# A pre-LN hedgehog attention and GeGLU block: statistics of one tile, transposes and applies moved between engines

## The chip, the cores and the metric

The kernel runs on one core of a Trainium2 chip. A core has TensorE (PE, matrix products and transposes), VectorE (DVE), ScalarE (ACT), GpSimd (POOL) and SyncE (SP, which here issues all the DMAs of the kernel's own code). Each engine works through its own list of instructions in order; engines wait for each other on semaphores. The metric is the device time of one execution in microseconds (us), as the median of several runs, lower is better.

## What is computed

The reference, cut to what matters. S = 2048 tokens, D = 640, H = 32 heads of Dh = 20, F = 1536, all bf16:

```python
x = A_x
h  = x + A_ref(layernorm(x), wqkv, w_phi, wo)
h2 = h + B_ref(layernorm(h), w_gate, w_up, w_down)
# A_ref
q, k, v = split(x @ wqkv)                         # H heads of 20
pq, pk = q @ w_phi[h], k @ w_phi[h]
phi_q = concat(softmax(pq), softmax(-pq))         # 40 features a head
phi_k = concat(softmax(pk), softmax(-pk))
kv, z = sum_s phi_k^T v, sum_s phi_k
o = (phi_q kv) / (phi_q z + 1e-6)
return o @ wo
# B_ref
return (gelu(x @ w_gate) * (x @ w_up)) @ w_down
```

There is no mask and no softmax over the sequence: the attention is linear, so kv and z are summed over all the tokens before the first query can be finished.

## The kernel before

The tokens are 16 tiles of 128, in four blocks of four (`x_sb[b]`). x is loaded, normalised (LN1) and transposed to `LN1T[b]`, which holds the features on the partitions; from it V, the K features and the Q features are made on TensorE. w_phi is folded into the K and Q weights on the chip: `BD` is w_phi set out as block diagonals, `fold` multiplies it with the transposed weights (`WkT`, `WqT`, transposed by DMA) and casts the product `wa` to `Wk2` or `Wq2`. All the code issues in program order, each engine keeping the order in which its instructions stand in the source; nothing is reordered. So a line moved in the source is moved in the list of each engine on which it issues something.

The opening (L249 to L440) brings the first tiles to the point where the loop can start. A layer norm has a statistics step, `ln_stats`: on DVE two `bn_stats` (L109) and a `bn_aggr` (L113) for each tile, then the reciprocal root of the variance, either on ScalarE as Ln and Exp (L118, L119, `log=True`) or on POOL as an addition and a power (L121, L122), and on POOL, where the apply is to be on ScalarE, the product mean times -rstd, `mr` (L127). Then there is an apply, on ScalarE (`ln_act`, L133) or on DVE (`ln_dve`, L138). The transposes are five on TensorE into a PSUM tile `tp` (L146), which ScalarE or DVE copies to LN1T (L147), or one DMA (L149). Tiles 0 and 1 (`CT`) are special: only their mean is subtracted (`xc`, L249) before the transposes, so that these need not wait for rstd, which comes in later as the scale of V's copy (`v_ev`, L292) and of K's exponentials (`k_tile`, L305; `nrstd` is -rstd). For the queries their part of LN1T is written again, normalised in full; this is the late apply in the loop's step 10. Tile 3's statistics come from ScalarE: `st3_act` makes the mean with an accumulating Identity and the sum of squares with an accumulating Square, and POOL makes the rstd (L377, L378); `ln_3` applies them on DVE. `warm` issues matmuls of ones. `v_part(t, c, ...)` multiplies feature blocks c of tile t with Wv.

The loop (L441 to L487) has one step for each tile t. Its order in a step:

- `k_tile(t)`: the K product `pk` on TensorE (L272), and on ScalarE the two exponentials `E` (L305, plus and minus).
- In steps 10 to 14 one `fold` of the query weights, whose cast to Wq2 is on ScalarE (L236).
- In steps 5, 9, 13 and 15 the sums kv of earlier tiles (`kv_tile`, `kvp`, L338).
- `v_mm(t + 4)`, the V product, then the apply of tile t + 6 on ScalarE with its DMA transpose, then the copy of V on ScalarE.
- In even steps the statistics of tiles t + 8 and t + 9, on DVE and POOL.
- `k_norm(t)`: on DVE the sums `sk` of the exponentials (L312) and their reciprocals `rs` (L316); then `vt` = V times rs for each of the two signs (L320), one on POOL and the other either on POOL at once (tiles in `VP` = 0, 2, 4, 6, 9, 11) or on DVE, one step later between that step's sk and rs (`todo`).
- In step 9 POOL sets up the masks (`KV`, `kmask`, L474 to L482). In step 10 the late apply of tiles 0 and 1, both on DVE, and their DMA transposes.
- In step 15 the query products of the first four groups, and their exponentials `Eq` (L363, L368). `QG` lists the groups: the number 5b + c stands for feature block c of token block b.

The last four tiles' `kv_tile` and the mask of kv end the loop. Then come the rest of the queries, attention (`attn_a` to `attn_e`: the products `ab` with KV, their copies `AB`, the division, Wo, the residual, LN2) and the FFN (`gate_up`, `down`), laid into each other by `weave`, which runs an attention step after a given number of FFN pieces.

PSUM tiles of the loop are taken from a pool `psG` of three buffers of two banks each: `pk`, `wa`, `pv` and `pq` in turn. So a product can begin when the one three before it has been read: for instance the wa of step 14 takes the buffer of step 13's pk, and the pk of step 15 that of step 13's wa.

Of the kernel before, what the change touches and what calls it, by code (L numbers as in the profile page):

```python
# [8 lines left out]
BF16 = mybir.dt.bfloat16  # L9
F32 = mybir.dt.float32  # L10
ALU = mybir.AluOpType
ACTF = mybir.ActivationFunctionType
# [5 lines left out]
def kernel(  # L18
# [12 lines left out]
    nc = tc.nc  # L31
    P = 128
    S = 2048
    D = 640
# [3 lines left out]
    NT = S // P  # L38
    NB = NT // 4
    NC = D // P  # L40
    NF = FF // P
    EPS = 1e-5
# [6 lines left out]
    LQ = (7, 8, 9, 9, 10)  # L49
    FQ = (10, 11, 12, 13, 14)  # L50

    QG = ((0, 1), (2, 3), (4, 5), (6,), (7, 8), (9, 10), (11, 12), (13, 14), (15,), (16,), (17,), (18,), (19,))
    QT = (15, 15, 15, 15)
    T3 = 3

# [11 lines left out]
    phi_v = A_w_phi.rearrange("h d f -> (h d) f")  # L67
# [8 lines left out]
    x_sb = [const.tile([P, 4, D], BF16, name=f"x_sb{b}") for b in range(NB)]  # L76
    wphi = const.tile([P, NC, Dh], BF16, name="wphi")
# [10 lines left out]
    nhalf = const.tile([P, 2], F32, name="nhalf")  # L88
# [52 lines left out]
    def transpose_to(dst, src, on_pe, on_dve=False):  # L141

        if on_pe:
            tp = psG.tile([P, 16, P], BF16, name="tp", tag="G")
            for c in range(NC):
                nc.tensor.transpose(tp[:, c, :], src[:, c * P:(c + 1) * P], ident)  # L146
            (nc.vector.tensor_copy if on_dve else nc.scalar.copy)(dst, tp[:, 0:NC, :])  # L147
        else:
            nc.sync.dma_start_transpose(dst, src)  # L149
# [7 lines left out]
    p1 = p1_cm.__enter__()  # L157
# [6 lines left out]
    fp = fp_cm.__enter__()  # L164
# [10 lines left out]
    nc.sync.dma_start(Wv[:, 0:2, :], w_v[:, 0:2, 2 * D:3 * D])  # L175
    nc.sync.dma_start(x_sb[0][:, 2:3, :], x_v[:, 2:3, :])
    nc.sync.dma_start(Wv[:, 2:4, :], w_v[:, 2:4, 2 * D:3 * D])
    nc.sync.dma_start(x_sb[0][:, 3:4, :], x_v[:, 3:4, :])
    nc.sync.dma_start(wphi, phi_v.rearrange("(c p) f -> p c f", p=P))
    nc.sync.dma_start(Wv[:, 4:5, :], w_v[:, 4:5, 2 * D:3 * D])  # L180
    nc.sync.dma_start(x_sb[1][:, 0:2, :], x_v[:, 4:6, :])

# [24 lines left out]
    def warm(*cols):  # L207
        for n in cols:
            nc.tensor.matmul(wu[:, 0, 0:n], lhsT=ones[:, 0:P], rhs=ones[:, 0:n], start=True, stop=True)
# [30 lines left out]
    lnp, Ek, Vt = {}, {}, {}  # L240
# [4 lines left out]
    def ln_0(t):  # L245
        xt, mean, rstd, _ = lnp[t] = ln_stats(p1, [x_sb[0][:, t, :]], f"c{t}", False, None, True)[0]
        nc.gpsimd.tensor_scalar(nrstd[t], rstd, -1.0, None, op0=ALU.mult)
        xc = fp.tile([P, D], BF16, name="xc", bufs=2)
        nc.vector.tensor_scalar(xc, xt, mean, None, op0=ALU.subtract)  # L249
        return xc  # L250

    def ln_st(*tiles, act=True, between=None, log=False):
        for t, v in zip(tiles, ln_stats(p1, [x_sb[t // 4][:, t % 4, :] for t in tiles], "1", act, between, log)):
            lnp[t] = v

    def ln_ap(t, on_act=False, on_pe=False):
        ln = (ln_act if on_act else ln_dve)(p1, "1", *lnp[t])
        if on_pe:
            lnp[t] = ln
        else:  # L260
            transpose_to(LN1T[t // 4][:, :, t % 4 * P:(t % 4 + 1) * P], ln, False)
# [20 lines left out]
    def v_part(t, *cs):  # L282

        if 0 in cs:
            pv[t] = gtile("pv")
        for c in cs:
            for u in range(2):
                nc.tensor.matmul(pv[t][:, u, 0:HD], lhsT=lnT(t, c), rhs=Wv[:, c, u * HD:(u + 1) * HD],
                                 start=(c == 0), stop=(c == NC - 1))
# [10 lines left out]
    def k_tile(t):  # L300
        pk = gtile("pk")
        proj(pk, t, Wk2, rows=t == 0)
        Ek[t] = ev.tile([P, 2, D], BF16, name="E", bufs=8)
        for s in range(2):
            nc.scalar.activation(Ek[t][:, s, :].rearrange("p (u f) -> p u f", u=2), pk[:, :, 0:HD],  # L305
                                 ACTF.Exp, scale=((lnp[t][2], nrstd[t]) if t in CT else (1.0, -1.0))[s])
# [60 lines left out]
        for s in signs:  # L367
            nc.scalar.activation(Eq[j][:, :, s, :], pqs[j][:, 0:len(QG[j])], ACTF.Exp, scale=(1.0, -1.0)[s])  # L368

    def st3_act(i):  # L370

        xt = x_sb[0][:, 3, :]
        if i == 0:
            nc.scalar.activation(sq3, xt, ACTF.Identity, scale=-1.0 / D, accum_out=v3[:, 0:1])
        else:
            nc.scalar.activation(sq3, xt, ACTF.Square, bias=v3[:, 0:1], accum_out=v3[:, 1:2])
            nc.gpsimd.tensor_scalar(v3[:, 2:3], v3[:, 1:2], 1.0 / D, EPS, op0=ALU.mult, op1=ALU.add)  # L377
            nc.gpsimd.tensor_tensor(v3[:, 3:4], v3[:, 2:3], nhalf[:, 0:1], op=ALU.pow)  # L378

    def ln_3():  # L380

        ln = lnp[3] = p1.tile([P, D], BF16, name="ln1", bufs=3)
        nc.vector.tensor_scalar(ln, x_sb[0][:, 3, :], v3[:, 0:1], v3[:, 3:4], op0=ALU.add, op1=ALU.mult)

    sq3 = fp.tile([P, D], BF16, name="sq3")
    v3 = fp.tile([P, 4], F32, name="v3")

    def bd(c0, c1):

        n = c1 - c0  # L390
        nc.vector.tensor_tensor(BD[:, c0:c1], wphi[:, c0:c1, None, :].to_broadcast([P, n, 8, Dh]),
                                hmask[:, c0:c1, :, None].to_broadcast([P, n, 8, Dh]), ALU.mult)

    def tr_c(t):
        transpose_to(LN1T[0][:, :, t * P:(t + 1) * P], xc[t], True, t == 1)

    xc = [ln_0(t) for t in CT[:1]]
    tr_c(0)
    xc.append(ln_0(1))
    warm(*[P] * 7)  # L400
    ln_st(2, act=False, log=True)
    v_part(0, 0, 1)
    tr_c(1)
    st3_act(0)
    v_part(0, 2, 3)
    ln_ap(2, on_pe=True)
    bd(0, NC)
    st3_act(1)
    v_part(1, 0, 1)
    ln_tp(2, True)  # L410
    v_part(1, 2, 3)
    v_part(0, 4)
    v_ev(0)
    v_part(1, 4)
    v_ev(1)
    ln_st(4, act=False)
    ln_3()
    v_part(2, *range(NC))
    v_ev(2)
    nc.sync.dma_start(x_sb[1][:, 2:4, :], x_v[:, 6:8, :])  # L420
# [21 lines left out]
    for t in range(NT):  # L442
        if t == T3:
            ps_cm.close()
            psG = ps_cm.enter_context(tc.tile_pool(name="psG", bufs=3, space=PSUM, reuse_waits="tile"))
            psK = ps_cm.enter_context(tc.tile_pool(name="psK", bufs=1, space=PSUM, reuse_waits="tile"))
            kvp = psK.tile([P, 2, 512], F32, name="kvp")
        k_tile(t)
        if t == 0:
            ln_ap(6)  # L450
        if t in FQ:
            fold(WqT, Wq2, True, [i for i, f in enumerate(FQ) if f == t])
        for j in range(len(QT)):
            if t == QT[j]:
                q_mm(j)
                q_exp(j)
        for i in KVG.get(t, ()):
            kv_tile(i)
        if 0 < t < NT - 4:
            v_mm(t + 4)  # L460
        if t > 0 and t + 6 < NT:
            ln_ap(t + 6, on_act=True)
        if 0 < t < NT - 4:
            v_ev(t + 4)
        if t % 2 == 0 and t + 8 < NT:
            ln_st(t + 8, t + 9)
        k_norm(t)
        load_T(WqT, 0, *[i for i, f in enumerate(LQ) if f == t])
        if t == 10:

            for i in CT:
                ln_ap(i)
        if t == 9:
            nc.gpsimd.memset(KV, 0.0)  # L474
            nc.gpsimd.memset(kmask, 1.0)
            for r in HALF:
                nc.gpsimd.affine_select(out=kmask[r], in_=kmask[r], pattern=[[4, NC], [-Dh, 4]],
                                        compare_op=ALU.is_ge, fill=0.0, base=0, channel_multiplier=1)
                nc.gpsimd.affine_select(out=kmask[r], in_=kmask[r], pattern=[[-4, NC], [Dh, 4]],
                                        compare_op=ALU.is_ge, fill=0.0, base=Dh - 1, channel_multiplier=-1)  # L480
            nc.gpsimd.tensor_copy(KV[:, :, 0, :, KC - 1], kmask)
            nc.gpsimd.tensor_copy(KV[:, :, 1, :, 0], kmask)  # L482
        if t == 13:
            nc.sync.dma_start(Wg, wg_v)
            nc.sync.dma_start(Wo, wo_v)
            nc.sync.dma_start(Wu, wu_v)
# [60 lines left out]
    def attn_a(t, dve=0):  # L547
        attn_a_mm(t)
        AB, ab = ABs[t % 2], st[t, "ab"]
        for u in ((1, 0) if t in (5,) else (0, 1)):  # L550
            (nc.vector.tensor_copy if u >= 2 - dve else nc.scalar.copy)(
                AB[:, :, u * UH:(u + 1) * UH].rearrange("p s h f -> p s (h f)"), ab[u][:, :, 0:UH * KC])
        st[t] = AB
# [215 lines left out]
    def attn_at(t, i, offs):  # L769

        fns = (attn_a, attn_b, attn_b2, attn_b3, attn_c, attn_d, attn_d2, attn_e)
        return [(i + o, fn, t) for fn, o in zip(fns, offs) if o >= 0]
# [5 lines left out]
    def attn_rest(t, i):  # L778
# [2 lines left out]


    weave(gus(0, 0, 256) + downs(0, (0, 1)),
          attn_at(2, 0, (-1, 0, 1, 2, 7, 7, 8, 10)) + attn_at(3, 1, (1, 2, 3, 4, 9, 9, 10, 12)) + attn_at(4, 6, SHORT2) + attn_at(5, 9, SHORT2) +
          attn_at(6, 13, SHORT2))
    weave(gus(0, 256, 512) + downs(0, (2, 3)),
          attn_at(7, 0, SHORT) + [(12, split), (14, attn_pair, 8), (16, attn_pair, 10)] + attn_rest(8, 15) +
# [37 lines left out]
```

## Time and profile before

| what | us |
|---|---|
| median of 3 runs | 277.09 (276.90 to 277.39) |
| the profiled execution | 277.39 |
| its span in the trace | 275.5 |
| opening, to the first pk | 0 to 16.56 |
| loop and end of kv | 16.56 to 70.3 |
| attention of all tiles and FFN | 70.3 to 275.5 |

The span is what the trace shows from the first to the last instruction; the 1.9 us between it and the execution's time lie around it. Times in the profile count from the span's start. The granted TensorE clock is 1.00 in the whole span by the records. Busy times of the engines by stretch, in us:

| stretch | TensorE | DVE | ScalarE | POOL |
|---|---|---|---|---|
| 0 to 6.2 | 5.34 | 3.64 | 2.52 | 2.78 |
| 6.2 to 16.55 | 10.30 | 8.66 | 7.50 | 2.65 |
| 16.55 to 70.3 | 53.24 | 51.35 | 45.69 | 40.63 |
| 70.3 to 272.7 | 201.66 | 112.85 | 83.65 | 51.13 |

A line such as `26.95 0.23 POOL L121 TENSOR_SCALAR ve<-mv ... x1` reads: start, duration, engine, line of the kernel, operation, what it writes and reads; in brackets what the engine waited for just before and how long. A duration includes time in which the instruction has been issued but cannot go on, so the same operation may be recorded with two durations. DVE's instructions overlap a little: sk to rs is 1.47 from start to start, rs to the next 0.47, a vt 0.765.

### The profile page before, as it was taken

The page shows a single profiled execution, that of the slowest core. Times are in us where ns is not written, and L with a number is a line of the kernel's source. Part 1 is how long each engine was busy: PE and PEld are TensorE (multiplying, and loading weights), DVE is VectorE, ACT ScalarE, POOL GpSimd, SP SyncE. Part 2 cuts the span into 40 slices and gives each one's busy share as a digit, 9 for nine tenths or more (in the row PEclk, how much of TensorE's full clock was granted, in tenths as well). Part 3 has the DMA queues.
Part 4 walks back from the last instruction along what each step waited for, and adds up shares of the span by engine and source line. Part 5 has one row for each costly group of instructions (what it writes and reads, how often), then busy time and mean ns, then how long its engine had stood idle before and what let it go on. Part 6 is the DMA issues. An engine that isn't in the chain of part 4 may idle for free.

```text
span 275.5 us, 5930 instructions
## 1 busy us (share of the span) xinstructions
PE 270.5 (98%) x2335; PEld 174.2 (63%) x2348; DVE 176.8 (64%) x335; ACT 139.4 (51%) x239; POOL 97.2 (35%) x218
## 2 busy tenths in 40 slices
PE   8999999999999999999999999999999999999995
PEld 5777767765455887788764555675555576444574
DVE  6889999999495776675478773356866333333322
ACT  4879898869489755374552345223245510223100
POOL 4248897765202317365312553101165300000000
PEclk9999999999999999999999999999999999999999
DMA  7973526589820021316111142110123111000011
GB/s 207 194 236 61 73 53 104 80 261 393 273 87 0 4 50 35 85 49 70 32 48 48 26 69 51 38 61 2 48 47 71 26 48 50 25 0 0 0 50 48
DMA packets 42235, 21.37 MB, mean 78 GB/s; under 512 B 35040, under 2 KB 40416, under 8 KB 42208
## 3 DMA queue, kind: packets, MB, share of 16 engines
q1 hardware_dynamic: 42208, 21.01, 31.1%
q8 instruction: 18, 0.29, 0.5%
q14 instruction: 9, 0.07, 0.1%
HBM read 10.18 MB, written 2.62 MB: 46 GB/s over the span
## 4 chain that ended last, share of the span: by engine, by line
PE 72%; DVE 13%; issue 7%; SPq 4%; DMA 2%; ACT 1%; POOL 1%; DVEq 0%; ACTq 0%; POOLq 0%
PE gu L663 37%; PE pd L682 19%; PE po L603 8%; DVE sk L312 6%; PE pq L363 5%; DVE rs L316 3%; DVE stats L109 3%; PE ab L531 2%; SPq L186 2%; DMA x_sb<-in_A_x_dram 2%; POOL vt L320 1%; DVE vt L320 1%; PE tp L146 0%; ACT L666 0%; DVE mv L113 0%
## 5 line engine op out<-in xcount | busy, mean ns | idle before, releaser
L666 ACT ACTIVATE g<-gu 128x512 bf16<-128x512 f32 (+1 forms) x60 | 30.7, 512 | 68.6 <-PE gu L663 68.4
L669 DVE TENSOR_TENSOR GT<-gu,g 128x512 bf16<-128x512 f32 (+1 forms) x60 | 34.5, 580 | 47.9 <-PE gu L663 39.3
L663 PE MATMUL gu<-LN2T,Wg 128*128 128x512 bf16 (+1 forms) x291 | 61.3, 335 | 0.5
L663 PE MATMUL gu<-LN2T,Wu 128*128 128x512 bf16 (+1 forms) x300 | 61.7, 336 | 0.0
L682 PE MATMUL pd<-Wd,GT 128*128 128x320 bf16 (+2 forms) x396 | 53.5, 295 | 0.0
L682 PEld LDWEIGHTS <-GT 128*128 128x128 bf16 x396 | 37.9, 98 | 14.7 <-DVE GT L669 0.2
L663 PEld LDWEIGHTS <-Wu 128*128 128x128 bf16 x300 | 29.4, 98 | 22.6
L663 PEld LDWEIGHTS <-Wg 128*128 128x128 bf16 x300 | 28.8, 98 | 21.4
L272 PEld LDWEIGHTS <-LN1T 128*128 128x128 bf16 x290 | 27.7, 98 | 10.8 <-DMA LN1T<-ln 0.3
L685 DVE TENSOR_TENSOR y<-pd,x_sb 128x320 bf16<-128x320 f32 (+2 forms) x29 | 13.9, 480 | 29.0 <-PE pd L682 29.0
L320 POOL TENSOR_TENSOR vt<-vS,rs 128x672 bf16<-128x672 bf16 x22 | 29.1, 1344 | 9.1 <-DVE rs L316 8.8
L603 PE MATMUL po<-Wo,oT 128*128 128x320 bf16 x160 | 24.3, 299 | 0.0
L272 PE MATMUL pk<-Wk,LN1T 128*128 128x320 bf16 x160 | 24.2, 299 | 0.0
L363 PE MATMUL pq<-LN1T,Wq 128*128 128x512 bf16 x96 | 22.9, 379 | 0.2
L312 DVE TENSOR_REDUCE sk<-E 128x64 f32<-128x1280 bf16 x16 | 22.9, 1431 | 0.0
L368 ACT ACTIVATE Eq<-pq 128x1024 bf16<-128x1024 f32 (+1 forms) x26 | 20.0, 830 | 1.7 <-PE pq L363 1.7
L603 PEld LDWEIGHTS <-oT 128*128 128x128 bf16 x160 | 15.6, 98 | 7.4 <-ACT oT L147 0.5
L305 ACT ACTIVATE E<-pk 128x640 bf16<-128x640 f32 x28 | 18.2, 707 | 3.9 <-PE pk L272 3.8
L272 PE MATMUL pv<-Wv,LN1T 128*128 128x320 bf16 x130 | 19.8, 299 | 0.0
L580 DVE TENSOR_TENSOR tt<-AB,w 128x1280 bf16<-128x1280 f32 x12 | 17.9, 1488 | 1.1 <-POOL w L573 0.9
L133 ACT ACTIVATE ln<-x_sb,v,rstd 128x640 bf16<-128x640 bf16 x14 | 12.9, 920 | 10.7 <-POOL v L642 10.3
L363 PEld LDWEIGHTS <-Wq 128*128 128x128 bf16 x100 | 9.4, 98 | 10.0
(110 smaller groups left out, 294.3 us busy)
## 6 DMA issues: line engine op xcount, KB each, us to landing
out_dram<-y SPq DMA_DIRECT2D x15, 160.0 KB, 1.8
Wg<-in_B_w_gate_dram SPq DMA_DIRECT2D x1, 1920.0 KB, 7.8
Wu<-in_B_w_up_dram SPq DMA_DIRECT2D x1, 1920.0 KB, 12.5
Wd<-in_B_w_down_dram SPq DMA_DIRECT2D x1, 1920.0 KB, 8.2
x_sb<-in_A_x_dram SPq DMA_DIRECT2D x2, 640.0 KB, 6.1
Wo<-in_A_wo_dram SPq DMA_DIRECT2D x1, 800.0 KB, 9.4
x_sb<-in_A_x_dram SPq DMA_DIRECT2D x4, 160.0 KB, 2.9
Wv<-in_A_wqkv_dram SPq DMA_DIRECT2D x2, 320.0 KB, 3.9
```

Of the source, the lines that this page charges most:

```text
L272: nc.tensor.matmul(ps[:, u, 0:HD], lhsT=lnT(t, c), rhs=W[:, c, u * HD:(u + 1) * HD], start=(c == 0), stop=(c == NC - 1))
L305: nc.scalar.activation(Ek[t][:, s, :].rearrange("p (u f) -> p u f", u=2), pk[:, :, 0:HD], ACTF.Exp, scale=((lnp[t][2], nrstd[t]) if t in C ...
L312: nc.vector.reduce_sum(sk, Ek[t].rearrange("p s (h f) -> p (s h) f", f=Dh), axis=AX.X)
L320: eng.tensor_tensor(vt[:, s], vS[t % 8], rs[:, s * H:(s + 1) * H, None].to_broadcast([P, H, VC]), ALU.mult)
L363: nc.tensor.matmul(pqs[j][:, i, :], lhsT=Wq2[:, kc, c * P:(c + 1) * P], rhs=LN1T[b][:, kc, :], start=(kc == 0), stop=(kc == NC - 1))
L368: nc.scalar.activation(Eq[j][:, :, s, :], pqs[j][:, 0:len(QG[j])], ACTF.Exp, scale=(1.0, -1.0)[s])
L580: nc.vector.tensor_tensor(tt.rearrange("p s (h f) -> p s h f", f=Dh), num, w[:, :, :, None].to_broadcast([P, 2, H, Dh]), ALU.mult)
L603: nc.tensor.matmul(pos[u], lhsT=st[t][:, c, :], rhs=Wo[:, c, u * HD:(u + 1) * HD], start=(c == 0), stop=(c == NC - 1))
L663: nc.tensor.matmul(gu[i][:, 0:n], lhsT=W[:, c, f * P:(f + 1) * P], rhs=LN2T[b][:, c, a0:a1], start=(c == 0), stop=(c == NC - 1))
L666: nc.scalar.activation(g[:, 0:n], gu[0][:, 0:n], ACTF.Gelu_apprx_tanh)
L669: nc.vector.tensor_tensor(st[b, "g", f][:, a0:a1], gu[1][:, 0:n], g[:, 0:n], ALU.mult)
L682: nc.tensor.matmul(ps, lhsT=st[b, "g", f][:, tl * P:(tl + 1) * P], rhs=Wd[:, f, f0:f1], start=(f == 0), stop=(f == NF - 1))
```

## The change

The statistics of tile 1 move from DVE to ScalarE and POOL (`st_act`, the former `st3_act` for any tile, with `xc_a` and `ln_a` for its subtraction and its apply on DVE). The transposes of tiles 0 and 1 follow one another, both copied to LN1T by DVE; three of seven warming matmuls go; the V parts stand in another order; BD is built in two pieces; w_phi is loaded ahead of x of tile 3. In the loop the apply of tile t + 6 stands ahead of k_tile(t) from t = 2 on, and so ahead of its exponentials on ScalarE; the statistics of a pair come one step earlier from the second pair on (in steps 1, 3 and 5 in place of 2, 4 and 6). In step 10 only tile 1 is applied again on DVE; tile 0 is applied on ScalarE in step 12, with a product mean times -rstd that POOL makes in step 10 after its vt. The query group with feature blocks 5 and 6 comes first. In the weave, the attention steps of tile 3 begin one FFN piece later, and the two copies of `ab` are swapped for tile 4 where they were for tile 5.

```diff
@@ -49,7 +49,7 @@
     LQ = (7, 8, 9, 9, 10)
     FQ = (10, 11, 12, 13, 14)
 
-    QG = ((0, 1), (2, 3), (4, 5), (6,), (7, 8), (9, 10), (11, 12), (13, 14), (15,), (16,), (17,), (18,), (19,))
+    QG = ((5, 6), (0, 1), (2, 3), (4,), (7, 8), (9, 10), (11, 12), (13, 14), (15,), (16,), (17,), (18,), (19,))
     QT = (15, 15, 15, 15)
     T3 = 3
 
@@ -175,8 +175,8 @@
     nc.sync.dma_start(Wv[:, 0:2, :], w_v[:, 0:2, 2 * D:3 * D])
     nc.sync.dma_start(x_sb[0][:, 2:3, :], x_v[:, 2:3, :])
     nc.sync.dma_start(Wv[:, 2:4, :], w_v[:, 2:4, 2 * D:3 * D])
+    nc.sync.dma_start(wphi, phi_v.rearrange("(c p) f -> p c f", p=P))
     nc.sync.dma_start(x_sb[0][:, 3:4, :], x_v[:, 3:4, :])
-    nc.sync.dma_start(wphi, phi_v.rearrange("(c p) f -> p c f", p=P))
     nc.sync.dma_start(Wv[:, 4:5, :], w_v[:, 4:5, 2 * D:3 * D])
     nc.sync.dma_start(x_sb[1][:, 0:2, :], x_v[:, 4:6, :])
 
@@ -367,23 +367,31 @@
         for s in signs:
             nc.scalar.activation(Eq[j][:, :, s, :], pqs[j][:, 0:len(QG[j])], ACTF.Exp, scale=(1.0, -1.0)[s])
 
-    def st3_act(i):
-
-        xt = x_sb[0][:, 3, :]
+    def st_act(t, i):
+
+        xt, v = x_sb[0][:, t, :], va[t]
         if i == 0:
-            nc.scalar.activation(sq3, xt, ACTF.Identity, scale=-1.0 / D, accum_out=v3[:, 0:1])
+            nc.scalar.activation(sqa, xt, ACTF.Identity, scale=-1.0 / D, accum_out=v[:, 0:1])
         else:
-            nc.scalar.activation(sq3, xt, ACTF.Square, bias=v3[:, 0:1], accum_out=v3[:, 1:2])
-            nc.gpsimd.tensor_scalar(v3[:, 2:3], v3[:, 1:2], 1.0 / D, EPS, op0=ALU.mult, op1=ALU.add)
-            nc.gpsimd.tensor_tensor(v3[:, 3:4], v3[:, 2:3], nhalf[:, 0:1], op=ALU.pow)
-
-    def ln_3():
-
-        ln = lnp[3] = p1.tile([P, D], BF16, name="ln1", bufs=3)
-        nc.vector.tensor_scalar(ln, x_sb[0][:, 3, :], v3[:, 0:1], v3[:, 3:4], op0=ALU.add, op1=ALU.mult)
-
-    sq3 = fp.tile([P, D], BF16, name="sq3")
-    v3 = fp.tile([P, 4], F32, name="v3")
+            nc.scalar.activation(sqa, xt, ACTF.Square, bias=v[:, 0:1], accum_out=v[:, 1:2])
+            nc.gpsimd.tensor_scalar(v[:, 2:3], v[:, 1:2], 1.0 / D, EPS, op0=ALU.mult, op1=ALU.add)
+            nc.gpsimd.tensor_tensor(v[:, 3:4], v[:, 2:3], nhalf[:, 0:1], op=ALU.pow)
+            lnp[t] = xt, None, v[:, 3:4], None
+
+    def ln_a(t):
+
+        ln = p1.tile([P, D], BF16, name="ln1", bufs=3)
+        nc.vector.tensor_scalar(ln, x_sb[0][:, t, :], va[t][:, 0:1], va[t][:, 3:4], op0=ALU.add, op1=ALU.mult)
+        return ln
+
+    def xc_a(t):
+
+        xc = fp.tile([P, D], BF16, name="xc", bufs=2)
+        nc.vector.tensor_scalar(xc, x_sb[0][:, t, :], va[t][:, 0:1], None, op0=ALU.add)
+        return xc
+
+    sqa = fp.tile([P, D], BF16, name="sqa")
+    va = {t: p1.tile([P, 4], F32, name=f"va{t}") for t in (1, 3)}
 
     def bd(c0, c1):
 
@@ -392,29 +400,33 @@
                                 hmask[:, c0:c1, :, None].to_broadcast([P, n, 8, Dh]), ALU.mult)
 
     def tr_c(t):
-        transpose_to(LN1T[0][:, :, t * P:(t + 1) * P], xc[t], True, t == 1)
-
-    xc = [ln_0(t) for t in CT[:1]]
+        transpose_to(LN1T[0][:, :, t * P:(t + 1) * P], xc[t], True, True)
+
+    st_act(1, 0)
+    xc = [ln_0(0)]
+    xc.append(xc_a(1))
     tr_c(0)
-    xc.append(ln_0(1))
-    warm(*[P] * 7)
+    tr_c(1)
+    st_act(1, 1)
+    nc.gpsimd.tensor_scalar(nrstd[1], lnp[1][2], -1.0, None, op0=ALU.mult)
+    warm(*[P] * 4)
     ln_st(2, act=False, log=True)
     v_part(0, 0, 1)
-    tr_c(1)
-    st3_act(0)
+    v_part(1, 0, 1)
+    bd(0, 2)
+    st_act(3, 0)
     v_part(0, 2, 3)
     ln_ap(2, on_pe=True)
-    bd(0, NC)
-    st3_act(1)
-    v_part(1, 0, 1)
+    bd(2, NC)
+    st_act(3, 1)
+    v_part(1, 2, 3)
     ln_tp(2, True)
-    v_part(1, 2, 3)
     v_part(0, 4)
     v_ev(0)
     v_part(1, 4)
     v_ev(1)
     ln_st(4, act=False)
-    ln_3()
+    lnp[3] = ln_a(3)
     v_part(2, *range(NC))
     v_ev(2)
     nc.sync.dma_start(x_sb[1][:, 2:4, :], x_v[:, 6:8, :])
@@ -445,6 +457,8 @@
             psG = ps_cm.enter_context(tc.tile_pool(name="psG", bufs=3, space=PSUM, reuse_waits="tile"))
             psK = ps_cm.enter_context(tc.tile_pool(name="psK", bufs=1, space=PSUM, reuse_waits="tile"))
             kvp = psK.tile([P, 2, 512], F32, name="kvp")
+        if t > 1 and t + 6 < NT:
+            ln_ap(t + 6, on_act=True)
         k_tile(t)
         if t == 0:
             ln_ap(6)
@@ -458,18 +472,19 @@
             kv_tile(i)
         if 0 < t < NT - 4:
             v_mm(t + 4)
-        if t > 0 and t + 6 < NT:
-            ln_ap(t + 6, on_act=True)
+        if t == 1:
+            ln_ap(7, on_act=True)
         if 0 < t < NT - 4:
             v_ev(t + 4)
-        if t % 2 == 0 and t + 8 < NT:
-            ln_st(t + 8, t + 9)
+        if t == 0 or t % 2 and t + 9 < NT:
+            ln_st(t + 9 - (t == 0), t + 10 - (t == 0))
         k_norm(t)
         load_T(WqT, 0, *[i for i, f in enumerate(LQ) if f == t])
         if t == 10:
-
-            for i in CT:
-                ln_ap(i)
+            nc.gpsimd.tensor_scalar(lnp[0][3], lnp[0][1], nrstd[0], None, op0=ALU.mult)
+            transpose_to(LN1T[0][:, :, P:2 * P], ln_a(1), False)
+        if t == 12:
+            ln_ap(0, on_act=True)
         if t == 9:
             nc.gpsimd.memset(KV, 0.0)
             nc.gpsimd.memset(kmask, 1.0)
@@ -547,7 +562,7 @@
     def attn_a(t, dve=0):
         attn_a_mm(t)
         AB, ab = ABs[t % 2], st[t, "ab"]
-        for u in ((1, 0) if t in (5,) else (0, 1)):
+        for u in ((1, 0) if t in (4,) else (0, 1)):
             (nc.vector.tensor_copy if u >= 2 - dve else nc.scalar.copy)(
                 AB[:, :, u * UH:(u + 1) * UH].rearrange("p s h f -> p s (h f)"), ab[u][:, :, 0:UH * KC])
         st[t] = AB
@@ -781,7 +796,7 @@
 
 
     weave(gus(0, 0, 256) + downs(0, (0, 1)),
-          attn_at(2, 0, (-1, 0, 1, 2, 7, 7, 8, 10)) + attn_at(3, 1, (1, 2, 3, 4, 9, 9, 10, 12)) + attn_at(4, 6, SHORT2) + attn_at(5, 9, SHORT2) +
+          attn_at(2, 0, (-1, 0, 1, 2, 7, 7, 8, 10)) + attn_at(3, 1, (2, 3, 4, 5, 9, 9, 10, 12)) + attn_at(4, 6, SHORT2) + attn_at(5, 9, SHORT2) +
           attn_at(6, 13, SHORT2))
     weave(gus(0, 256, 512) + downs(0, (2, 3)),
           attn_at(7, 0, SHORT) + [(12, split), (14, attn_pair, 8), (16, attn_pair, 10)] + attn_rest(8, 15) +
```

## The prediction

> **What bounds the kernel now.** I read the engine shares first, then the chain of waits, then the timeline around the few waits that the chain shows. The page and the waits view:
>
> ```profile
> span 275.5 us, 5930 instructions
> PE 270.5 (98%) x2335; PEld 174.2 (63%) x2348; DVE 176.8 (64%) x335; ACT 139.4 (51%) x239; POOL 97.2 (35%) x218
> PE 72%; DVE 13%; issue 7%; SPq 4%; DMA 2%; ACT 1%; POOL 1%; DVEq 0%; ACTq 0%; POOLq 0%
> ...
> PE kvp L338 <- POOL vt L320: 0.5, 1, 0.5
> ```
>
> TensorE is busy for 98% of the span, so a gain has to remove TensorE time or a TensorE wait, and there is little of either. Yet 13% of the chain is DVE: in the K/V loop the chain runs on another engine. The chain's pieces at the two ends of the loop, and the timeline there:
>
> ```profile
> 11.93 4.59 DMA x_sb<-in_A_x_dram
> ...
> 67.15 0.55 DVE rs L316
> ...
> 67.86 1.98 POOL vt L320
> ...
> 16.55 0.89 DVE L109 BATCH_NORM_STATS2 stats<-x_sb 128x6 f32<-128x320 bf16 x2 [0.60 <-DMA x_sb<-in_A_x_dram]
> ...
> 69.88 0.38 PE L338 MATMUL kvp<-vt,E 128*64 128x84 bf16 x10 [0.45 <-POOL vt L320]
> ```
>
> The chain enters DVE at 16.55, when tiles 6 and 7 land, stays there to 67.15, and hands over to POOL's last vt, for which TensorE waits 0.45. From there on it is TensorE. So through the loop DVE and TensorE are level within 0.45 us: work that delays TensorE by d costs d − 0.45, and work that delays DVE and POOL costs all of it.
>
> Two engines that get in each other's way decide the rest. The timeline at tiles 1 and at 9 to 14:
>
> ```profile
> 26.95 0.23 POOL L121 TENSOR_SCALAR ve<-mv 128x2 f32<-128x2 f32 x1
> 27.82 0.85 DVE L320 TENSOR_TENSOR vt<-vS,rs 128x672 bf16<-128x672 bf16 x1
> ...
> 51.52 2.17 DVE L138 TENSOR_SCALAR ln<-x_sb,mvc,rstdc 128x640 bf16<-128x640 bf16 x2
> 52.27 0.83 POOL L474 MEMSET KV<- 128x880 bf16 x1
> ...
> 54.09 0.70 ACT L236 CAST Wq<-wa 128x640 bf16<-128x640 f32 x1
> 54.66 1.33 ACT L305 ACTIVATE E<-pk 128x640 bf16<-128x640 f32 x2
> 54.69 1.32 POOL L320 TENSOR_TENSOR vt<-vS,rs 128x672 bf16<-128x672 bf16 x1
> 55.00 1.72 DVE L320 TENSOR_TENSOR vt<-vS,rs 128x672 bf16<-128x672 bf16 x1
> 55.84 0.74 ACT L236 CAST Wq<-wa 128x640 bf16<-128x640 f32 x1
> 57.81 0.48 PE L227 MATMUL wa<-BD,WqT 128*128 128x140 bf16 x6
> ```
>
> A vt on DVE takes 0.85 alone (27.82) but 1.72 when POOL's vt is running (55.00): DVE stands until 0.13 before POOL's ends. The pair of L138 takes 2.17 against 0.43 each alone; it stood through a vt and a memset of POOL.
>
> **The change part by part.**
>
> *Opening* (tile 1's statistics on ScalarE, both transposes together, three warming matmuls fewer, another order of the V parts). Two bn_stats and one aggregate leave DVE (0.88 + 0.21); two accumulating ScalarE passes come (0.74 + 0.18 and 0.83 + 0.19, as tile 3's at 7.72 and 8.59), and POOL's scale and power (0.19 + 0.57). On TensorE the wait before tile 1's V parts (0.2 at 7.98) and three warms of 128 columns (0.107 each at the pace of that time) go, so tile 2's transposes come some 0.4 earlier. Then tile 3 is late. Its x is sent behind wphi (issue to issue 0.43 to 0.5: landing at about 8.2 for 7.70), its two ScalarE passes now stand behind tile 2's Ln and Exp and end at about 10.0, POOL's power at 10.9, DVE's L384 at 11.4, and its transposes start at 11.4 to 11.5 where they start at 11.26. That makes the first pk 0.1 to 0.25 late (16.56). DVE's chain starts with the landing at 16.52, whose issue at 11.93 stands on SP's queue behind the five transposes of WkT (5.20 to 11.89) as before, so it neither gains nor loses. TensorE's 0.1 to 0.25 goes into the wait found below. I count the opening as 0; without that cover it would cost up to 0.25, and its best end is −0.45, if TensorE gained 0.4 to the end of the opening and kept it.
>
> *Statistics of a pair one tile earlier* (10/11, 12/13, 14/15 before tiles 1, 3, 5). Nothing is added. But POOL's ve, rstd and two mr of the pair (26.95 to 29.03) now run ahead of its vt of tile 1 instead of during DVE's. Walk it from row starts: DVE's rs of tile 0 at 22.30; statistics to 24.5 (1.77, as at 24.70 to 26.47); sk and rs of tile 1 to 26.5; sk of tile 2 to 27.85. POOL: vt of tile 0 twice, 23.0 to 25.55; the four small ones 1.5, to 27.1; vt of tile 1 from 27.1 to 28.4. DVE's vt of tile 1, ready at 27.8, can start only at 28.25: 0.45 lost, where 27.82 shows none lost. The same walk gives 0.41 at tile 3 and 0.35 at tile 5. Sum 1.2; if each POOL piece is a little later, up to 0.65, 0.6, 0.5, which is 1.7; nothing is lost if DVE's instruction gets in first. DVE and POOL both reach tile 6 by s = 1.2 later. DVE has no idle time before there that could take it up.
>
> *ScalarE applies ahead of the exponentials.* Same instructions; the 0.92 of an apply (pitch 0.81) now stands before E, which waits for pk anyway. The next ln is one tile earlier, and the 0.74 that ScalarE stood at 41.52 for POOL's mr goes. ScalarE is 51% busy: I take 0 on the path.
>
> *Late apply.* Tile 1's stays on DVE (0.43, with its wait); tile 0's leaves DVE, 0.35 to 0.43 gained there, and comes on ScalarE at tile 12, between the Wq cast at 54.09 and the E pair of tile 13 at 54.66. It needs the new mean·(−rstd) of POOL, one small operation (0.24 to 0.26, as an mr), issued at tile 10 behind POOL's vt of that tile, which ran from 54.69 to 56.01. Even with the times of before: product done at 56.2, apply 56.25, E of tile 13 from 57.06 to 58.36 (it ended at 55.99), the Wq cast after it to 58.95 (56.58). TensorE's wa of tile 14 started at 57.81 into the buffer that this E frees: 0.55 late; pk of tile 15 at 58.12 into the buffer that the cast frees: 0.87 late. Against the 0.45 of TensorE's slack: +0.42, had POOL not been late. With s on POOL, 0.42 + 1.2 = +1.6. And there is a race: with s less the 0.35 to 0.43 saved, DVE's vt of tile 10 (55.00) asks at about 55.87, POOL's (54.69) at 55.90. If POOL wins, the sum stands at 1.6. If DVE wins, POOL waits 0.65 to 0.75 more, and all of that is in the product's time: 2.3. Of the two, 0.03 us apart, no row decides; I take the middle, 1.95.
>
> What is queued behind the waiting apply on ScalarE: both E of tile 13, the cast, then E of tiles 14 and 15. DVE's sk of tile 13 (59.10) waits for the first of these, and TensorE for all.
>
> [...] L138's first instruction, issued at 51.52 during POOL's vt, took 1.816: it stood not only through that vt, to 52.33, but through the memset that came after it, to 53.1. [...]
>
> *Order of the query groups, the weave of the first attention tiles.* The first q group now is one that does not read block 0, whose tile 0 is transposed about 3 us later than before (53.40 + 2.5); q starts after 60, so nothing waits. The KV readings of tile 3 move behind the third gate_up; TensorE lost 0.11 about 92.96, where the activation table's load and the first gelu hold it: −0.1, bounds −0.2 and +0.2.
>
> Sum: opening 0, statistics and late apply +1.95, weave −0.1: +1.85. The profiled execution took 277.39 with a span of 275.5 (1.9 around it); the median is 277.09, so the sum made against the span is put on the median: 277.09 + 1.85 = 278.94, say 279.0.
>
> **The rivals.**
> 1. *Faster, by the DVE work removed.* If the vts don't meet (DVE's gets in ahead of POOL's) and POOL's product is done by 54.8, DVE's chain loses 0.35 to 0.43, TensorE's wait of 0.45 shrinks with it, and opening and weave give 0.1 to 0.3: 277.09 − 0.45 − 0.2 = 276.4 to 276.6. For it: DVE has the longest unbroken stretch of the chain. Against it: POOL's vt of tile 10 ran to 56.01, 1.2 after ScalarE is free.
> 2. *No change.* The vts don't meet, but the product is late: +0.42 − 0.1, so 277.4.
> 3. *Slower, DVE the bound.* The apply is early enough after all, the vts meet: 1.2 − 0.4 = +0.8, so 277.9. It decides if the product is ready by 54.8 + s.
> 4. *Slower, the clock.* TensorE's pace goes from 107 to 56 ns per 128 columns between 6.45 and 6.68; with ten transposes in place of seven warms and five, the release could come later. V and pk up to 16.56 at half pace for another 1.3 or so, of which the wait above hides half: +0.7, so 279.7. [...]
>
> **How the numbers follow.** This kernel's runs differ by up to 0.2% (0.55 us), so "same" is 276.54 to 277.64. My forecast 0.58, rival 1 0.14, rival 2 0.12, rival 3 0.06, rival 4 0.10. Slower: 0.74; same 0.12; faster 0.14. The likeliest has 278.3 to 279.6 (1.6 and 2.3, 0.2 either way, and 0.3 for s up to 1.7). To leave out 2 in 10 at most, the range has to reach over rivals 2 to 4: 277.0 to 280.2.
>
> **What would show it.** In the timeline of after: ScalarE's L133 for tile 0 at about 57.5 to 58.3 with 2.5 us or more idle before it, released by POOL's L484; E of tile 13 ending at 59.6 to 60.4; TensorE's wa of tile 14 waiting two microseconds or more for ScalarE; kvp at the end of the loop no longer waiting for POOL. DVE's vt of tiles 1, 3, 5 recorded at 1.2 to 1.5 for 0.85. Tiles 6 and 7 still landing at 16.5; first pk at 16.65 to 16.8. It is wrong if the vts keep 0.85, if L484 runs before 55, or if ScalarE's apply starts with no wait.

## The result

The changed kernel takes 280.42 us (median of 4 runs, 280.30 to 281.36) against 277.00 for the kernel before beside it: a ratio of 1.0123, 95% interval 1.0108 to 1.0138. It is slower by 3.4 us, where the prediction said 1.9 and ended its range at 280.2. Two later comparisons of the same kernels gave 1.0129 (1.0097 to 1.0161) and 1.0139 (1.0119 to 1.0158); with more executions the kernel before had medians of 277.34 to 277.48, so 277.00 is at its low end. The profiled execution of the changed kernel took 281.36 with a span of 279.3, 3.8 more than the span before.

From the page of the changed kernel: the span, the busy times, and TensorE's granted clock in 40 slices of 7 us (tenths of full speed).

```profile
span 279.3 us, 5939 instructions
PE 272.8 (98%) x2345; PEld 174.4 (62%) x2345; DVE 176.3 (63%) x333; ACT 140.2 (50%) x241; POOL 96.7 (35%) x221
PEclk9999999988999999999999999999999999999999
```

TensorE's busy time rose by 2.3, though it has three matmuls less to do; and in the slices from 56 to 70 us the clock is down, where the page before has a 9 in every slice. The timeline of the changed kernel there, and below it the pk of the kernel before:

```profile
55.91 0.84 DVE L320 TENSOR_TENSOR vt<-vS,rs 128x672 bf16<-128x672 bf16 x1
55.94 1.98 POOL L320 TENSOR_TENSOR vt<-vS,rs 128x672 bf16<-128x672 bf16 x1
57.90 0.30 POOL L484 TENSOR_SCALAR mrc<-mvc,nrstd 128x1 f32<-128x1 f32 x1
58.24 0.92 ACT L133 ACTIVATE ln<-x_sb,mrc,rstdc 128x640 bf16<-128x640 bf16 x1 [3.38 <-POOL mrc L484]
59.07 1.27 ACT L305 ACTIVATE E<-pk 128x640 bf16<-128x640 f32 x2
60.39 0.47 PE L227 MATMUL wa<-BD,WqT 128*128 128x140 bf16 x6 [2.35 <-ACT E L305]
60.98 2.83 PE L272 MATMUL pk<-Wk,LN1T 128*128 128x320 bf16 x10
```

```profile
56.44 1.53 PE L272 MATMUL pk<-Wk,LN1T 128*128 128x320 bf16 x10
```

Read downward, the first block is the chain that the prediction described: DVE's vt of tile 10 came 0.03 us ahead of POOL's, POOL's took 1.98 instead of 1.31, the product (`mrc`) followed at 57.90, ScalarE had stood 3.38 for it, E of tile 13 came after the apply, and TensorE stood 2.35 for E. Its last line is the new thing: ten matmuls of pk took 2.83, where the same ten took 1.52 or 1.53 in the steps before it. The windows view of the changed kernel, with the stretch, its length, busy times and counts of TensorE, weight loads, DVE, ScalarE and POOL, then the granted clock:

```profile
57.00:64.60 7.60, 5.14 (x27) 2.79 (x26) 6.34 (x8) 5.22 (x9) 6.28 (x6) 0.78 0.49 128
61.00:64.40 3.40, 3.40 (x12) 1.70 (x12) 3.40 (x4) 2.27 (x4) 2.08 (x2) 0.51 0.83 221
```

For the 3.4 us after the wait TensorE had half its clock. From 60.98 to 63.60 ten matmuls of pk went at 267 ns from start to start (136 before), and the first pq until 64.4 at 376 to 427 ns (216): 1.6 us on top of the wait.

This is the profiled execution, and not every execution has it. Half the clock for 3.4 of 279 us by itself brings the mean granted clock of an execution to 0.994. Of the four executions measured here only the profiled one (281.36, span 279.3) has 0.994; the other three (280.30 to 280.48, spans 278.2 to 278.4) have 1.000. In the three measurements of the changed kernel together, 8 of 14 executions have 0.993 or 0.994, with a median of 281.5, and 6 have 1.000, with a median of 280.4. So the 280.42 is a time at full clock, and the clock is not what puts it above the forecast. Against 277.42, the median of 69 executions of the kernel before in the later measurements, the change costs 3.0 at full clock and 4.1 where the clock falls.

### The profile page after: what moved, and what is told of

Same layout as the page of the kernel before. It is cut to its first block, busy times and chain, and to the rows that moved or that the text cites. A ratio compares the mean times of both kernels' runs of the same rounds, so it can differ in the third digit from the quotient of the medians.

```text
span 279.3 us, 5939 instructions
## 1 busy us (share of the span) xinstructions
PE 272.8 (98%) x2345; PEld 174.4 (62%) x2345; DVE 176.3 (63%) x333; ACT 140.2 (50%) x241; POOL 96.7 (35%) x221
## 3 DMA queue, kind: packets, MB, share of 16 engines
HBM read 10.18 MB, written 2.62 MB: 46 GB/s over the span
## 4 chain that ended last, share of the span: by engine, by line
PE 77%; DVE 12%; issue 3%; POOL 3%; DMA 2%; ACT 2%; SPq 1%; DVEq 0%; POOLq 0%
PE gu L678 37%; PE pd L697 19%; PE pq L363 8%; PE po L618 8%; DVE sk L312 4%; DVE stats L109 3%; PE ab L546 3%; DVE rs L316 2%; DMA x_sb<-in_A_x_dram 2%; POOL vt L320 1%; PE pk L272 1%; PE kvp L338 1%; PE tp L146 1%; DVE vt L320 1%; DVE mv L113 1%
## 5 line engine op out<-in xcount | busy, mean ns | idle before, releaser
L272 PEld LDWEIGHTS <-LN1T 128*128 128x128 bf16 x290 | 28.3, 99 | 11.4 <-issue 0.2
L320 POOL TENSOR_TENSOR vt<-vS,rs 128x672 bf16<-128x672 bf16 x22 | 29.9, 1372 | 11.0 <-DVE rs L316 8.2
L272 PE MATMUL pk<-Wk,LN1T 128*128 128x320 bf16 x160 | 25.5, 310 | 0.1
```

Of the source, the lines that this page charges most:

```text
L272: nc.tensor.matmul(ps[:, u, 0:HD], lhsT=lnT(t, c), rhs=W[:, c, u * HD:(u + 1) * HD], start=(c == 0), stop=(c == NC - 1))
L320: eng.tensor_tensor(vt[:, s], vS[t % 8], rs[:, s * H:(s + 1) * H, None].to_broadcast([P, H, VC]), ALU.mult)
```

## The experiments

The loads of the opening landed at different times from run to run, so the loop began at different times with one and the same opening: BD's first piece, which needs w_phi, began at 7.20 without a wait in the run with both applies on DVE, at 7.93 after 0.28 of waiting for that load in the changed kernel and at 8.29 after 0.77 in the run with the early product. To compare loops, I read three starts in each trace: sk of tile 0 on DVE (where the loop's DVE chain begins), the end of E of tile 13, and the start of the last kvp matmul. The difference of the first and the last is the length of the loop, free of the opening.

| kernel | ratio to before, 95% interval | sk of tile 0 | E of 13 ends | last kvp | loop | E of 13 to last kvp |
|---|---|---|---|---|---|---|
| before | 1 | 20.83 | 55.99 | 70.06 | 49.23 | 14.07 |
| changed | 1.0123 (1.0108 to 1.0138) | 20.40 | 60.34 | 73.90 | 53.50 | 13.56 |
| changed, second time | 1.0129 (1.0097 to 1.0161) | 20.80 | 60.79 | 74.26 | 53.46 | 13.47 |
| changed, third time | 1.0139 (1.0119 to 1.0158) | 20.54 | 60.49 | 73.98 | 53.44 | 13.49 |
| product early | 1.0035 (1.0018 to 1.0052) | 20.91 | 57.18 | 71.10 | 50.18 | 13.92 |
| apply on DVE | 1.0052 (1.0029 to 1.0075) | 20.91 | 56.52 | 71.80 | 50.89 | 15.28 |
| statistics late | 1.0045 (1.0030 to 1.0061) | 20.21 | 58.47 | 70.39 | 50.18 | 11.92 |
| early product, late statistics | 1.0008 (0.9994 to 1.0021) | 21.71 | 58.27 | 70.89 | 49.19 | 12.62 |
| opening alone | 1.0013 (1.0001 to 1.0025) | 21.04 | 56.11 | 70.28 | 49.23 | 14.17 |
| old opening, rest repaired | 1.0006 (0.9993 to 1.0019) | 20.99 | 57.54 | 70.17 | 49.19 | 12.63 |
| filled wait | 1.0106 (1.0079 to 1.0132) | 21.47 | 61.41 | 73.33 | 51.86 | 11.92 |
| filled wait, second time | 1.0124 (1.0102 to 1.0145) | 20.53 | 60.51 | 72.42 | 51.89 | 11.91 |
| filled, no added tile | 1.0129 (1.0108 to 1.0149) | 21.86 | 61.79 | 73.71 | 51.86 | 11.92 |
| filled in part | 1.0104 (1.0084 to 1.0123) | 21.44 | 61.38 | 73.30 | 51.86 | 11.92 |

**The clock: matmuls of zeros in the wait.** Before the fold of step 14 in the changed kernel (`zeros` is a tile of its own, set to 0 by DVE in the opening):

```diff
+        if t == 14:
+            for i in range(14):
+                nc.tensor.matmul(kvp[:, 0, 0:420], lhsT=zeros[:, 0:P], rhs=ones[:, 0:420], start=False, stop=False,
+                                 skip_group_check=True)
```

> The changed kernel with 14 TensorE matmuls of zeros (420 columns, some 0.175 us each, 2.45 us in all, added to kvp as nothing) between the pk and the wa of step 14, where TensorE stood for 2.5 us. ScalarE's wait and the end of that wait stay as they are. Theory (the wait was long enough to take TensorE's clock down, and pk of step 15 and the first pq ran at half pace for it): pk of step 15 back to 136 ns a matmul, 1.8 us less, 278.6 us. Rival (the half pace has to do with what else runs then, or the loss is the wait alone): 280.4 us, pk of step 15 still at 267 ns.

Measured: 280.48, the rival's time, but with pk of step 15 at 136 ns, the theory's pace. Beside the changed kernel in one measurement:

> The kernel with 14 matmuls of zeros in TensorE's long wait, once more beside the changed kernel on the same chip. Theory (the wait takes the clock down): 1.2 to 1.8 us below the changed kernel in the same call, pk of step 15 at 136 ns. Rival (the loss is the wait alone): within 0.4 us of it.

> The changed kernel as it is, on the same chip and beside the same runs of the kernel before as the next three, since the loads of the opening landed up to 0.7 us apart from one run to the next. Theory: 3.4 us above the kernel before, as the first time. Rival (a slower chip of itself): less than 2.5 or more than 4.5.

Measured: 280.77 filled, 281.02 not, by the medians the rival. With the zeros of KV in place of a tile of its own, whole and in part, and the changed kernel beside them:

```diff
+                nc.tensor.matmul(kvp[0:Dh, 0, 0:420], lhsT=KV[:, 0, 0, 0, 0:Dh], rhs=ones[:, 0:420], start=False, stop=False,
+                                 skip_group_check=True)
```

> The changed kernel with 14 filling matmuls in TensorE's wait as before, but with the zeros of KV as the stationary operand, so that no tile is added and nothing moves in SBUF. Theory (clock): granted clock 1.00 from 57 to 65 us, kvp ends 1.6 us earlier than in the changed kernel, and of that 1.0 to 1.6 us are left at the end. Rival (the time saved is lost again to later transposes by DMA, which the first two fills showed twice, 0.4 to 0.56 us): less than 0.5 us left at the end.

> The same with 6 filling matmuls, 1.1 us, so that 1.4 to 2.2 us of TensorE's wait are left. What decides is whether such a wait still takes the clock down; the runs so far show 1.0 us (kept) and 2.5 us (down). If it does: pk of step 15 at 267 ns, the changed kernel's time. If not: 136 ns and the time of the full fill.

> The changed kernel beside the two fills on the same chip: 3.4 us above the kernel before by both theories, with the granted clock at about 0.5 for 3.4 us after the wait.

Measured: 280.97 (14 matmuls), 280.26 (6), 281.32 (unchanged, half clock in all four executions). With 14, 0.35 is left at the end, the rival's outcome; with 6, 1.1, and the remaining wait kept the clock. TensorE's timeline and the windows of the run with 6:

```profile
58.21 1.24 PE L467 MATMUL kvp<-const-bfloat16-1.0,KV 128*20 128x420 bf16 x6
61.43 0.47 PE L227 MATMUL wa<-BD,WqT 128*128 128x140 bf16 x6 [1.98 <-ACT E L305]
62.02 1.52 PE L272 MATMUL pk<-Wk,LN1T 128*128 128x320 bf16 x10
...
57.00:64.60 7.60, 5.51 (x38) 3.15 (x36) 6.33 (x9) 5.32 (x9) 6.28 (x7) 1.00 0.45 91
61.00:64.40 3.40, 2.86 (x21) 1.81 (x21) 2.99 (x4) 3.40 (x7) 2.08 (x3) 1.00 0.70 130
```

The wait for E is still there, and pk is back at 1.52 with a clock of 1.00. In all four filled runs the time from E of 13 to the last kvp is 11.92 or 11.91; unfilled it is 13.47 to 13.56. So where the clock falls it costs 1.55 to 1.65, and filling TensorE's time with useless work took that away and left the wait for E where it was. None of the 20 filled executions has a mean clock of 0.994, against 8 of 14 unfilled ones. On the medians less of it is seen: 1.1 with 6 matmuls, 0.25 and 0.35 with 14. For one, the unfilled kernel does not always pay it: three of the six executions behind the 281.02 have a clock of 1.000 (279.49 to 280.52). For another, in the three profiles with 14 the part behind the loop is 0.5 to 1.0 longer (205.9 to 206.4 from the last kvp to the end of the span, 205.4 unfilled): there TensorE waited 0.4 by the waits view for oT, an attention tile transposed by DMA, at about 133 us (and 0.25 more at 107 in one of them); the run with 6 and the unfilled ones have no such wait. And the loop began 0.9 and 1.3 later in the filled profiles of the third measurement than in the unfilled one. Why those landings were late is open.

**The late product alone, and the collisions alone.** Three edits of the changed kernel, each taking one delay out:

```diff
+        if t == 8:
+            nc.gpsimd.tensor_scalar(lnp[0][3], lnp[0][1], nrstd[0], None, op0=ALU.mult)
         if t == 10:
-            nc.gpsimd.tensor_scalar(lnp[0][3], lnp[0][1], nrstd[0], None, op0=ALU.mult)
```

> The changed kernel with POOL's product for the late apply of tile 0 issued in step 8 instead of step 10, where POOL has free time (49.7 to 51.0). Theory (the whole loss is ScalarE's wait for that product and what follows on TensorE): the apply at 54.9, E of step 13 ends at 57.0, TensorE waits for neither wa nor pk, no half pace, and kvp's last wait for POOL is smaller too: 276.5 us (276.2 to 277.0). Rival (the waits of DVE's vt in tiles 1, 3 and 5, 1.7 us in all, are what sets the end): 278 us or more, with TensorE waiting for POOL's vt at the last kvp.

Measured: 278.52 against 277.48. The rival's number, and its wait: the apply started at 55.05 without waiting, TensorE did not wait at step 14, and the last kvp waited 0.79 for POOL's vt. DVE's collisions now set the end.

```diff
-            nc.gpsimd.tensor_scalar(lnp[0][3], lnp[0][1], nrstd[0], None, op0=ALU.mult)
+            ln_ap(0)
...
-        if t == 12:
-            ln_ap(0, on_act=True)
```

> The changed kernel with tile 0's late apply back on DVE in step 10, and no product on POOL. Leaves opening, statistics one step earlier and applies ahead of the exponentials. Theory (ScalarE's wait is the whole loss): no wait of TensorE at wa of step 14; DVE's extra L138 costs up to 0.43 at the end of the loop: 277.4 us (277.0 to 278.0). Rival (collisions of the vts decide): 278.3 us or more.

Measured: 278.71 against 277.48, again the rival. Without the late product and with both applies on DVE as before, the loop is 1.66 longer than before: that is the price of the collisions (with the applies ahead of the exponentials, which this run keeps). The run with the early product has 0.71 less; I put that down to the apply that DVE lost, which no run shows by itself. One of this run's twelve executions (281.14) has a mean clock of 0.994 too; it has no trace. The collisions are seen in tile 1's vt in the changed kernel; the prediction's fence shows the same instruction at 0.85:

```profile
26.84 1.31 POOL L320 TENSOR_TENSOR vt<-vS,rs 128x672 bf16<-128x672 bf16 x1
27.39 1.47 DVE L320 TENSOR_TENSOR vt<-vS,rs 128x672 bf16<-128x672 bf16 x1
28.79 0.54 DVE L316 RECIPROCAL rs<-sk 128x64 f32<-128x64 f32 x1
```

DVE's vt was issued at 27.39, within POOL's (26.84 to 28.15), and the next rs began 1.40 after it instead of 0.765: 0.63 lost. At tiles 3 and 5 the same two starts are 1.38 and 1.24 apart, 0.61 and 0.47 lost, 1.71 in all, which the 1.66 bears out. The next run does too: it moves the statistics alone, and its loop of 50.18 is 1.68 shorter than the 51.86 of the changed kernel at full clock (filled).

```diff
-        if t == 0 or t % 2 and t + 9 < NT:
-            ln_st(t + 9 - (t == 0), t + 10 - (t == 0))
+        if t % 2 == 0 and t + 8 < NT:
+            ln_st(t + 8, t + 9)
```

> The changed kernel with the statistics of pairs in steps 2, 4 and 6 again. The product for the late apply stays behind POOL's vt of step 10, which now comes some 1.2 to 2 us earlier: E of step 13 ends at about 58.2, TensorE waits 0.3 to 0.9 and keeps its pace. Theory (a wait below a microsecond costs its length, the long one its length and the clock): 277.4 us (277.0 to 277.9), DVE's vt of tiles 1, 3 and 5 at 0.85 again. Rival (the statistics' place doesn't matter): 280.4 us.

Measured: 278.70 against 277.48, between the two. Its timeline has the waits of the theory:

```profile
54.03 0.84 DVE L320 TENSOR_TENSOR vt<-vS,rs 128x672 bf16<-128x672 bf16 x1
54.07 1.98 POOL L320 TENSOR_TENSOR vt<-vS,rs 128x672 bf16<-128x672 bf16 x1
...
56.37 0.92 ACT L133 ACTIVATE ln<-x_sb,mrc,rstdc 128x640 bf16<-128x640 bf16 x1 [1.61 <-POOL mrc L484]
...
58.52 0.47 PE L227 MATMUL wa<-BD,WqT 128*128 128x140 bf16 x6 [0.59 <-ACT E L305]
...
59.10 1.52 PE L272 MATMUL pk<-Wk,LN1T 128*128 128x320 bf16 x10
```

A wait of 0.59, pk at full pace, DVE's vts of tiles 1, 3 and 5 at 0.85; the loop is 0.95 longer than before. DVE's vt of tile 10 is ahead of POOL's here too, since DVE has one apply less, and POOL's takes 1.98. This profile had the earliest sk of all, and its execution, 277.87, was the fastest of its twelve, so the median of 278.70 is likely to hold later openings as well.

So with either delay taken out the loop is still 0.95 longer (50.18 twice, against 49.23); with both in it is 2.63 longer at full clock (51.86, filled) and 4.2 where the clock falls. They add more than their sum because they are in line: the collisions make POOL late, POOL makes the product late, and the wait, 2.35 instead of 0.59, can then take the clock.

**What is left without both.**

> The changed kernel with POOL's product in step 8 and the statistics of pairs in steps 2, 4 and 6: neither the late product nor the collisions are left. Theory (these two are two separate delays, of which the longer sets the end): no wait of TensorE in the loop but a small one for POOL's last vt; 277.3 us (276.9 to 277.8), against 277.5 before. Rival (the opening or the order in the attention cost something of their own): 278.2 us or more.

Measured: 277.76 against 277.34, inside the theory's range; the edits are the first and the third above. And the opening by itself (loop and attention as in the kernel before):

> The kernel before with the opening of the changed one alone (tile 1's statistics on ScalarE, both transposes together, the loads' order), loop, query groups and attention as before. Theory (the opening gains DVE some 0.4 us where the loads are early and loses as much where wphi lands late, since BD stands ahead of tile 2's apply on DVE): 277.6 us (277.2 to 278.3) against 277.5. Rival (a gain, since DVE's first statistics of tile 6 came at 16.1 for 16.5): 277.0 or less.

Measured: 277.64 against 277.34, inside the theory's range and at the edge of what can be told apart. Its loop is 49.23 long, the same as before. In the twelve profiles with the new opening sk of tile 0 began at 20.21 to 21.86, on average 20.99; in the two with the old one at 20.83 and 20.99. A gain of the new opening isn't seen.

Then the old opening with all that is left of the change:

```diff
+        if t > 1 and t + 6 < NT:
+            ln_ap(t + 6, on_act=True)
         k_tile(t)
...
-        if t > 0 and t + 6 < NT:
-            ln_ap(t + 6, on_act=True)
+        if t == 1:
+            ln_ap(7, on_act=True)
...
-            for i in CT:
-                ln_ap(i)
+        if t == 8:
+            nc.gpsimd.tensor_scalar(lnp[0][3], lnp[0][1], nrstd[0], None, op0=ALU.mult)
+        if t == 10:
+            ln_ap(1)
+        if t == 12:
+            ln_ap(0, on_act=True)
```

> The kernel before with what is left of the change when its two delays are taken out: late apply of tile 0 on ScalarE in step 12 with POOL's product in step 8, applies ahead of the exponentials, new order of the query groups and of the attention; the opening and the statistics' steps as before. Theory (DVE saves one L138 of 0.43 and TensorE its wait of 0.45 for POOL's last vt): 0.3 to 0.5 us below the kernel before. Rival (other waits take its place, or the attention's order costs something): 0.2 us or less below it, or above it.

Measured: 277.65 against 277.47, no difference that can be told. The theory failed. TensorE's wait at the last kvp did go, and POOL's last vt ended 48.27 after sk of tile 0 instead of 48.99; but the timeline of this run shows what came in its place:

```profile
34.56 0.97 POOL L127 TENSOR_SCALAR mr<-mv,rstd 128x1 f32<-128x1 f32 x2
...
35.34 0.92 ACT L133 ACTIVATE ln<-x_sb,mr,rstd 128x640 bf16<-128x640 bf16 x1 [1.07 <-POOL mr L127]
37.49 0.70 PE L272 MATMUL pv<-Wv,LN1T 128*128 128x320 bf16 x4 [0.75 <-ACT E L305]
```

An apply that stands ahead of E must have its mr by then. With the statistics in the old steps it hasn't, so E stands behind an apply that waits, and TensorE behind E. The earlier statistics were there for the earlier applies; both parts belong together, and the pair pays with collisions. A kernel with the late apply and early product alone, applies and statistics in their old places, has not been measured, so whether that beats the kernel before is open.

In this run and in the one with both delays removed, 0.2 of the difference to the kernel before lies around the span, where no view reaches: execution less span is 2.03 to 2.14, in the kernel before 1.78 to 1.91. The changed kernel has it too (2.02 to 2.11); the run with both applies on DVE and the one with the opening alone don't (1.80 to 1.89). Its cause is open.

## Why the prediction failed, step by step

- *Who sets the end.* Right: with both delays TensorE, waiting for E of tile 13. The wait was to be two microseconds or more; it was 2.35. ScalarE's apply was to start at 57.5 to 58.3 after standing 2.5 or more; it started at 58.24 after 3.38. E was to end at 59.6 to 60.4; it ended at 60.34. That these fell inside is partly luck, since the loop began 0.43 earlier than in the kernel before: counted from sk of tile 0, E of 13 ended at 39.94, where the forecast comes to 38.77 to 39.57.
- *The race at tile 10.* Reckoned as 55.87 for DVE and 55.90 for POOL, it came as 55.91 and 55.94, and DVE won. The order is as reckoned; the times agree because the early opening hid that DVE and POOL had lost more by then than the 1.2 of the reckoning. The forecast took the middle, 1.95; the upper case, 2.3, was what happened.
- *The step that failed:* the term "statistics and late apply +1.95" was too small. In the loop at full clock it measured 2.63 (51.86 in the filled runs, against 49.23). The mechanism was the one described and two sizes in it were off: the collisions took 1.71 where 1.2 was reckoned, and the race went to its upper case where the middle was taken. With these two the prediction's own sum, 0.42 + 1.7 + 0.7 = 2.8, comes near. Its range did reach over them; what it left out is the time around the span, taken as the same 1.9 for both and 0.2 longer in the changed kernel. With the 0.08 that the part behind the loop gained, that makes 2.75 of the 3.0 at full clock; the executions at full clock have no trace without filling, and the last 0.25 stays open. The 277.00 of the first comparison, 0.4 below the later medians, does the rest of the 3.4.
- *A cost that the sum did not have:* "work that delays TensorE by d costs d − 0.45". It holds for a delay that leaves TensorE's pace alone. In the 8 of 14 executions where the clock fell, 3.4 us at half clock cost more: 1.55 to 1.65 in the three that were traced, 1.1 between the medians. In the profiled one the loop is 4.27 longer, 2.63 and 1.64; its opening was 0.43 earlier, the part behind the loop 0.08 shorter, and so the spans differ by 3.8. Rival 4 had a clock effect in the opening, where none showed (V's matmuls come 136 ns apart from 6.36 on, in the kernel before from 6.68 on), and no run shows the 1.3 more at half pace that it reckoned with; I did not ask what a long wait does to the clock in the middle of the kernel. By the rows it went down after waits of 2.35, 2.62 and 3.13 (the three profiles of the changed kernel; before the last, one of ten matmul records is missing) and stayed up after 1.98 and 0.59.
- *The collisions.* Right in kind and place; reckoned at 1.2 with 1.7 as the upper end, measured at 0.63 + 0.61 + 0.47 = 1.71, and the loop with the collisions alone is 1.66 longer.
- *The late product without collisions*, 0.42 reckoned, came to 0.95 in the loop's length. I had set the race at tile 10 against the collisions only; it comes without them too (54.03 and 54.07), and 0.42 with POOL's vt 1.98 long for 1.32 is 1.08.
- *The opening*, counted as 0 with up to 0.25: pk of tile 0 started at 16.80, at the end of the forecast 16.65 to 16.8, but at 16.46 and 16.66 in the other two profiles of the same kernel, so the hit says little. That tiles 6 and 7 land at 16.5 in any case was wrong: statistics of tile 6 began between 15.9 and 17.5 in the runs with the new opening.
- *The weave*, −0.1: right. From the start of the last kvp to the end of the span it is 205.48 and 205.46 in the two profiles with the old order of query groups and attention, and 205.38 to 205.40 in nine with the new one (the three with 14 fills aside): 0.08 gained, which the loop's loss hides.

## What to carry to other kernels

A new wait of a saturated TensorE may cost more than its length: here one of 2.35 us brought 3.4 us at half clock with it, 1.6 us more, in some executions and not in others. So look at the granted clock in the window after it, and at the mean clock of every execution before the profile of one is taken for the median of all. Two delays that each look small have to be priced together where one feeds the other. And a small operation that another engine waits for should stand ahead of the long one in its queue: here the same product two steps earlier on POOL took the wait away.

## What was not expected of the hardware

TensorE's clock halved after a single wait of 2.35 us in a kernel that kept it busy at 98%, and came back 3.4 us later (61.0 to 64.4 in the first run). With six useless matmuls in the wait (1.24 us together), which left 1.98 of waiting, it stayed at full speed. By the clock records the changed kernel's profiled execution has full clock from 6.32 to 60.93, half of it to 64.34 and full again from there; the kernel before has full clock from 6.63 on (ahead of that there is no record, so the 1.00 given for the whole span before begins there). The 3.41 us before the fall and the slow ones after it:

```profile
57.52:60.93 3.41, 1.00 (x10) 0.60 (x9) 2.15 (x3) 2.69 (x5) 3.41 (x5) 1.00 0.17 33
60.93:64.34 3.41, 3.37 (x12) 1.72 (x12) 3.41 (x4) 2.28 (x4) 2.09 (x2) 0.50 0.84 219
```

The wait of 2.35, from 58.04 to 60.39, lies in the first line; the fall came 0.54 after its end. In the other two profiles of the changed kernel, with waits of 2.62 and 3.13, the clock from 61.00 to 64.40 was 0.50 and 0.53. It was 1.00 there with the wait of 1.98 and with that of 0.59, and the run with both applies on DVE, where TensorE waited 0.7 and 0.8 for vts at the end of the loop, has a mean clock of 1.000. No wait between 1.98 and 2.35 has a trace, nor has an unfilled execution of the changed kernel at full clock; what decides, and why the same kernel pays in 8 of 14 executions, is not shown.

And with one opening the loop began anywhere in 1.65 us (sk of tile 0 at 20.21 to 21.86 in twelve profiles), which is half of what the change cost; in the run of 20.21 BD had waited 0.28 for the load of w_phi, in the filled run of 21.47 it had waited 1.01.
